# Attention's reads of PSUM traced with a raised priority

## The chip, the cores and the metric

The kernel runs on one core of one Trainium2 chip. The metric is the device time of one execution in microseconds (us); lower is better. Engines are named as the profile names them: PE (TensorE, matmuls), DVE (VectorE), ACT (ScalarE), POOL (GpSimd) and SP (SyncE, which here only issues DMAs). PSUM is the memory that matmuls write; it is split into banks of 512 float32 per partition.

## The reference

Two parts follow each other: causal attention with a bias, and a layer that mixes tokens by a Fourier transform and then applies an MLP. Cut to what matters:

```python
scores = q @ k^T / sqrt(D)                            # 8 batches, 8 heads, 576 tokens, D = 64
cum = cumsum(max(s, 0)); bias = -(cum[:, None] - cum[None, :])
scores = where(causal, -1e9, scores + min(bias, 0))
attn = exp(scores - max(scores)); attn /= sum(attn) + 1e-9
x = attn @ v                                          # heads side by side: (8, 576, 512)
u = x + real(fft(fft(x, axis=tokens), axis=features))
un = (u - mean(u)) / sqrt(var(u) + 1e-6)
out = u + relu(un @ w_ch1) @ w_ch2                    # 512 -> 2048 -> 512
```

The weights come in as float64 words, which the kernel turns into float32 and then into a high and a low part, so that three float32r matmuls give nearly float32 precision.

## The kernel before

Attention works on 32 pairs of heads (`i` = 0 to 31, four pairs to a batch). Each pair has generators: `high` and `low` split q and k into parts (L404, L420); `maxes` multiplies q by k in blocks of 128 queries and takes each row's maximum from PSUM with DVE (L456, read at L459 and L463), then transposes the maxima on PE (L468), copies them out with ACT (`mt`, L470) and sends them by DMA into a row of the next product; `scores` multiplies k by q with the bias and the maximum inside the product (L488, L489), and ACT takes the exponential out of PSUM into `P` (L492); `av` multiplies by V (L520), and ACT copies the product out (L523, L524, L526); `recip` inverts the row sums (L535, L536), sends them to DRAM (`rd`, L538) and reads them back spread over partitions (`rb`, L541); `finish` scales the product (`xa` or `xr`, L556) and moves part of it by DMA into `xs` (L558 to L560).

In the loop of L582 the generators of neighbouring pairs are woven: `scores(i)`, `av(i - 1)`, `maxes(i + 1)`, `high(i + 2)`, `recip(i - 2)` and `finish(i - 2)` run side by side. Every fourth pair a batch is complete, and `folds` forms sums and differences of it (`Aw`, `Bw`, `Df` on DVE and POOL; high and low parts `De`, `Do`, `eh` by a cast on ACT and a subtraction on DVE, through `split`, L67). `fourier` (L273) then runs its matmuls (pzs, pzc, pyc, pys) between those of attention, and adds the result into `xa` and `xs` on POOL (L321 to L324), from where DMAs write it to DRAM (L326 to L328).

The weights have 16 chunks. Six are converted to float32 during attention (`convert_w`, stored as `wD`); the other ten are converted in the first of nine MLP tiles, four quarters a chunk: L82, L84, L86 and L87 on DVE, L83 and L111 on ACT, L88 on POOL, and L113 half on DVE and half on POOL. An MLP tile is 16 steps of 24 matmuls (L182, and L195 to L197 one step later), with a relu on ACT (`zh`, L186) and its remainder on DVE (`zl`, L187) between. `ln_tile` prepares the tokens of a tile (L126 to L159); its last step on DVE is a reciprocal over 128x512 (L158).

What sets the order: each engine works through one queue in order. The order is made when the kernel is built. For PE it is the written order from L581 to L636 (`manual_schedule`), so through the whole attention loop. For DVE, ACT, POOL and SP a scheduler chooses among the instructions that it holds ready, by a priority that counts up as instructions are traced; the lower number goes first. The pools decide who waits: exponentials and Fourier products share three banks (`ps`), maxima and products with V five (`psm`).

Of the kernel before, what the change touches and what calls it, by code (L numbers as in the profile page):

```python
# [10 lines left out]
AF = mybir.ActivationFunctionType  # L11
ALU = mybir.AluOpType
# [3 lines left out]
AX = mybir.AxisListType  # L16
# [9 lines left out]
NEG = -1.0e30  # L26
# [3 lines left out]
N0 = 3  # L30
N1 = 8
WEXP = 0x38000000 + (20 << 20)

# key chunks: (keys, first query of the product, queries of the product, first query kept)
CH = [(128, 0, 576, 0), (128, 128, 448, 128), (128, 256, 320, 256), (128, 320, 256, 384), (64, 320, 256, 512)]
# [5 lines left out]
def fused_kernel(ctx, tc, qkT, vA, sP, wP, tabD, tabS, corr, out):  # L41
# [23 lines left out]

    # ---------------------------------------------------------------- MLP
    def split(dst_h, dst_l, src):  # L67
# [5 lines left out]
    def rounded(pool, f, x, bufs):  # L73
        """256 columns of chunk f of both weights, from the words of their float64, rounded to nearest: generates, returns the f32."""
        m = pool.tile([128, WC], I32, tag="wm", name="wm", bufs=bufs)
        raw = pool.tile([128, 2 * WC], I32, tag="raw", name="raw", bufs=bufs)
        nc.sync.dma_start(out=raw, in_=wP[f, :, WC * x:WC * x + WC].bitcast(I32))
        hi = raw.rearrange("p (n w) -> p n w", w=2)[:, :, 1]
        lo = raw.bitcast(U16).rearrange("p (n w) -> p n w", w=4)[:, :, 1]
        yield 0.0  # L80
        e = pool.tile([128, WC], I32, tag="we", name="we", bufs=bufs)
        nc.vector.tensor_scalar(e, hi, 0x7FF00000, None, op0=ALU.bitwise_and)  # L82
        nc.scalar.activation(e, e, AF.Relu, bias=wbias, scale=8.0)  # L83
        nc.vector.tensor_scalar(m, hi, 0xFFFFF, 0x100000, op0=ALU.bitwise_and, op1=ALU.bitwise_or)  # L84
        yield 0.4
        nc.vector.scalar_tensor_tensor(out=e, in0=hi, scalar=-0x80000000, in1=e, op0=ALU.bitwise_and, op1=ALU.bitwise_or)  # L86
        nc.vector.scalar_tensor_tensor(out=m.bitcast(F32), in0=lo, scalar=2.0 ** -16, in1=m, op0=ALU.mult, op1=ALU.add)  # L87
        nc.gpsimd.tensor_mul(e.bitcast(F32), m.bitcast(F32), e.bitcast(F32))  # L88
        yield 0.4
        return e.bitcast(F32)  # L90

    def convert_w(pool, lo, hi, bufs):
        """Chunks lo..hi-1 as f32, into wD."""
        for f in range(lo, hi):
            for x in range(1024 // WC):
                m = yield from rounded(pool, f, x, bufs)
                nc.sync.dma_start(out=wD[f, :, WC * x:WC * x + WC], in_=m)
                yield 0.2

    def load_w(pool, f):  # L100
        """Chunk f of both weights in high and low parts: into W."""
        wh = pool.tile([128, 1024], F32R, tag=f"wh{f}", name=f"wh{f}")
# [13 lines left out]
    def spread_sum(t, name, n):  # L116
        """1/512 of the sum of t over the partitions, on every partition (PSUM)."""
        th = lnp.tile([128, TOK], F32R, tag="th", name="th")
        tl = lnp.tile([128, TOK], F32R, tag="tl", name="tl")
        split(th[:, :n], tl[:, :n], t[:, :n])  # L120
        m = bank(name)
        nc.tensor.matmul(m[:, :n], ones, th[:, :n], start=True, stop=False)
        nc.tensor.matmul(m[:, :n], ones, tl[:, :n], start=False, stop=True)
        return m

    def ln_tile(t0, n, lag):  # L126
        """Centred tokens in high and low parts, their mean and 1 / deviation: generates into LN."""
        u = lnp.tile([128, 4, TOK], F32, tag="u", name="u")
# [84 lines left out]

    # ---------------------------------------------------------------- Fourier mixing
    fft_ctx = ExitStack()
# [27 lines left out]
    def folds(b, xa, xs):  # L243
        """The even and odd parts of one batch; xa: rows 0..255 of x^T, xs: rows 512-p and 384-p."""
        De = [fft.tile([128, 2, 289], F32R, tag=f"De{i}", name=f"De{i}") for i in range(2)]
# [27 lines left out]
    def fourier(b, xa, xs):  # L273
        """Fourier mixing of one batch in place."""
        De, Do = folded.pop(b)
# [66 lines left out]

    # ---------------------------------------------------------------- attention
    attb_ctx, att_ctx, atop_ctx = ExitStack(), ExitStack(), ExitStack()
# [4 lines left out]

    # Products of width 128: rows 0..2 carry the running sum (high, low) and the maximum,  # L350
    # rows 3..63 are zero, rows 64..127 carry the high parts of q and k.
    R = NB * NH
# [51 lines left out]
    def high(i):  # L404
        """The high parts of q and k, the running sums, and no maximum yet."""
        st = sts[i]
# [13 lines left out]
    def low(i):  # L420
        """The low parts of q and k, each beside the high part of the same."""
        st = sts[i]
# [20 lines left out]
    def maxes(i):  # L443
# [4 lines left out]
        for h in range(2):  # L448
            for c in range(5):
# [4 lines left out]
                for x, (k0, n) in enumerate(parts):  # L454
                    p = psm.tile([128, 512], F32, tag="m", name="pm", bufs=5)
                    nc.tensor.matmul(p[:nq, :n], qy[:, h, 128 * c:128 * c + nq], ky[:, h, k0:k0 + n], start=True, stop=True)  # L456
                    if len(parts) > 1 and not x:
                        first = M1[:nq, h:h + 1]
                        nc.vector.tensor_reduce(out=first, in_=p[:nq, :n], axis=AX.X, op=ALU.max)  # L459
                    else:  # L460
                        n = nk - k0
                        m0 = 512 - 128 * c + k0
                        nc.vector.tensor_tensor_reduce(out=trash[:nq, :n], in0=p[:nq, :n], in1=amask[:nq, m0:m0 + n], scale=1.0,  # L463
                                                       scalar=first if x else NEG, op0=ALU.add, op1=ALU.max, accum_out=col)
                    yield 1.0
# [10 lines left out]
    def scores(i):  # L476
# [3 lines left out]
        for h in range(2):  # L480
            P = attb.tile([128, PW], F32, tag="P", name="P", bufs=4)
            st["P"].append(P)
            for c, (nk, q0, nq, qk) in enumerate(CH):
                ksl = slice(128 * c, 128 * c + nk)
                parts = [(0, 256), (256, 320)] if c == 0 else [(q0, nq)]
                for a, n in parts:
# [4 lines left out]
                    o = POFF[c] + lo - qk  # L491
                    nc.scalar.activation(P[:nk, o:o + a + n - lo], p[:nk, lo - a:n], AF.Exp, scale=0.125)  # L492
                    if c == 3:
# [9 lines left out]
    def av(i):  # L503
# [5 lines left out]
        for h in range(2):  # L509
            P = st["P"][h]  # L510
            vs = slice(64 * h, 64 * h + 128)
            for lo, n, tg in ((0, 256, "A"), (256, 320, "B")):
                p = psm.tile([128, 512], F32, tag="m", name="pav" + tg, bufs=5)
                cs = [c for c in range(5) if CH[c][3] < lo + n]
                for c in cs:
# [5 lines left out]
                    if c == cs[-1]:  # L521
                        if h:
                            nc.scalar.copy(r1[:, lo:lo + n], p[0:1, :n])  # L523
                            nc.scalar.copy(x[64:128, lo:lo + n], p[64:128, :n])  # L524
                        else:
                            nc.scalar.copy(x[:, lo:lo + n], p[:, :n])  # L526
                    yield 4 * w / 2.4
            # the sums of P, the second head's beside a row of their own
            nc.sync.dma_start(out=sums[16 * h:16 * h + 16], in_=r1 if h else x[64:65])
# [90 lines left out]

    # ---------------------------------------------------------------- MLP over all tokens
    zp = ctx.enter_context(pool("zp"))
# [49 lines left out]
def take(gen, quota):  # L672
    """The part of a generator up to a cost."""
    done = 0.0
# [24 lines left out]
def weave(*streams):  # L699
    """Runs generators side by side, each at the pace of its total cost."""  # L700
    for _ in mixed(*streams):
        pass
# [105 lines left out]
```

## Time and profile before

| What | us |
|---|---|
| Median of three timed runs | 1434.8 |
| Lowest and highest of them | 1433.98 and 1438.31 |
| Profiled execution, its span (the page gives no other time for it) | 1440.3 |
| PE busy in it | 1336.1 |
| DVE busy | 749.1 |
| POOL busy | 555.6 |
| ACT busy | 539.6 |

The profiled execution is one more run; it lies 5.5 us above the median of the timed ones. Attention starts its first exponentials at 25 us and takes about 17 us a pair; the last pair starts at 544 us. From there to 720 us the end of attention, the last Fourier mixing and the conversion of ten weight chunks overlap with the first MLP tile. From 720 us on PE runs the remaining eight tiles with hardly a gap. A row of the timeline gives start, duration, engine, line, operation, output<-input, sizes, and in brackets the idle time ahead of it with who ended it. A row of the waits gives who waited for whom, the total, how often, and the longest.

### The profile page before, as it was taken

To read this page: it belongs to the slowest core of one execution; us is meant where nothing else is said; L and a number is where in the kernel's file an instruction comes from. 1 tells how busy PE (TensorE), PEld (TensorE's weight loads), DVE (VectorE), ACT (ScalarE), POOL (GpSimd) and SP (SyncE) were. 2 spreads that over 40 slices of the span, in tenths; PEclk is the share of its full clock that TensorE was granted. 3 is DMA by queue.
4 is the path that set the end of the run, shared out by engine and by line. 5 is a ranking of instruction groups with operands and counts; after the bars stand their busy time and mean duration, and the time that the engine had idled before them with its cause. 6 is when DMAs were issued, how large, how long until landed. Compare 5 with 4: busy or idle time off the path is not lost.

```text
span 1440.3 us, 17967 instructions
## 1 busy us (share of the span) xinstructions
PE 1336.1 (93%) x6190; PEld 1073.6 (75%) x6190; DVE 749.1 (52%) x1684; ACT 539.6 (37%) x1211; POOL 555.6 (39%) x540
## 2 busy tenths in 40 slices
PE   4987989897989897998799999999999999999998
PEld 2766767686867685786588888888888888888886
DVE  6667676867676778789833332133321323212212
ACT  4775656565656557344412121121211212112110
POOL 6454465655555566565641400314013140123300
PEclk9998989999989998899899999999999999999999
DMA  8655556565655545533200000000000000000000
GB/s 216 163 144 145 156 151 176 145 163 168 154 158 140 164 118 166 172 119 116 94 23 30 30 30 8 22 30 30 30 8 22 30 30 30 8 22 0 30 0 30
DMA packets 78166, 124.98 MB, mean 87 GB/s; under 512 B 11256, under 2 KB 36185, under 8 KB 78075
## 3 DMA queue, kind: packets, MB, share of 16 engines
q1 hardware_dynamic: 75627, 119.83, 28.8%
q0 software_dynamic: 1632, 2.43, 0.9%
q10 hardware_dynamic: 816, 1.57, 0.3%
q8 instruction: 49, 0.80, 0.2%
q14 instruction: 42, 0.34, 0.1%
HBM read 76.78 MB, written 23.07 MB: 69 GB/s over the span
## 4 chain that ended last, share of the span: by engine, by line
PE 50%; DVE 7%; POOL 2%; DMA 1%; issue 1%; ACT 1%; SPq 0%; DVEq 0%; POOLq 0%; ACTq 0%
PE h L182 25%; PE acc L197 8%; PE acc L195 8%; PE acc L196 8%; POOL we L88 1%; DVE wm L87 1%; DVE wm L84 1%; DVE we L82 1%; DVE wl L113 1%; DVE we L86 1%; DVE ucl L147 0%; DVE Df L259 0%; POOL wl L113 0%; DMA raw<-in_wP_dram 0%; ACT wh L111 0%
## 5 line engine op out<-in xcount | busy, mean ns | idle before, releaser
L187 DVE SCALAR_TENSOR_TENSOR zl<-h,zh 128x512 fp32r<-128x512 f32 x144 | 98.7, 686 | 405.6 <-ACT zh L186 405.6
L186 ACT ACTIVATE zh<-h 128x512 fp32r<-128x512 f32 x144 | 85.9, 596 | 531.7 <-PE h L182 531.7
L197 PE MATMUL acc<-zl,wh 128*128 128x512 f32 x576 | 227.5, 395 | 3.9 <-DVE zl L187 3.9
L195 PE MATMUL acc<-zh,wh 128*128 128x512 f32 x576 | 227.8, 396 | 1.2 <-ACT zh L186 1.2
L196 PE MATMUL acc<-zh,wl 128*128 128x512 f32 x576 | 226.9, 394 | 0.0
L520 PE MATMUL pavB<-P,va 128*128 128x320 f32 (+2 forms) x640 | 201.7, 404 | 7.8 <-ACT stage L524 7.1
L456 PE MATMUL pm<-KQ 128*128 128x256 f32 (+4 forms) x384 | 159.5, 434 | 38.5 <-DVE Mx L463 16.2
L492 ACT ACTIVATE P<-ps 128x320 f32<-128x320 f32 (+4 forms) x384 | 144.9, 390 | 116.7 <-PE ps L489 111.9
L488 PE MATMUL ps<-KQ 128*128 128x256 f32 (+3 forms) x384 | 153.0, 401 | 21.6 <-ACT P L492 12.8
L182 PE MATMUL h<-uch,wh 128*128 128x512 f32 x576 | 159.2, 397 | 8.3 <-ACT wh L111 8.3
L182 PE MATMUL h<-uch,wl 128*128 128x512 f32 x576 | 157.9, 396 | 0.8 <-DVE wl L113 0.8
L182 PE MATMUL h<-ucl,wh 128*128 128x512 f32 x576 | 157.2, 394 | 0.0
L463 DVE CUSTOM_DVE_ANT_0 trash<-pm,amask 128x128 bf16<-128x128 f32 (+3 forms) x256 | 123.8, 484 | 39.8 <-PE pm L456 23.3
L211 POOL TENSOR_TENSOR o<-o,w 128x512 f32<-128x512 f32 x32 | 41.6, 1301 | 251.6 <-issue 217.8
L182 PEld LDWEIGHTS h<-uch,wh 128*128 128x128 f32 x576 | 107.8, 189 | 35.8 <-ACT wh L111 11.9
L197 PEld LDWEIGHTS acc<-zl,wh 128*128 128x128 f32 x576 | 108.8, 189 | 30.9 <-DVE zl L187 5.8
L520 PEld LDWEIGHTS pavB<-P,va 128*128 128x128 f32 (+1 forms) x640 | 107.5, 198 | 32.4 <-issue 12.5
L182 PEld LDWEIGHTS h<-uch,wl 128*128 128x128 f32 x576 | 108.7, 189 | 26.6 <-DVE wl L113 1.5
L195 PEld LDWEIGHTS acc<-zh,wh 128*128 128x128 f32 x576 | 108.7, 189 | 26.4 <-ACT zh L186 2.1
L182 PEld LDWEIGHTS h<-ucl,wh 128*128 128x128 f32 x576 | 108.9, 189 | 24.7
L196 PEld LDWEIGHTS acc<-zh,wl 128*128 128x128 f32 x576 | 108.8, 189 | 24.8
L489 PE MATMUL ps<-q,k 128*128 128x256 f32 (+3 forms) x384 | 120.9, 317 | 1.4 <-POOL q L435 1.4
(139 smaller groups left out, 2035.1 us busy)
## 6 DMA issues: line engine op xcount, KB each, us to landing
qk<-in_qkT_dram SPq DMA_DIRECT2D x32, 576.0 KB
raw<-in_wP_dram SPq DMA_DIRECT2D x64, 256.0 KB
va<-in_vA_dram SPq DMA_DIRECT2D x32, 480.0 KB
q<-KQ SPq DMA_DIRECT2D x32, 288.0 KB
k<-KQ SPq DMA_DIRECT2D x32, 288.0 KB
rb<-rd SPq DMA_DIRECT2D x64, 144.0 KB
u<-uD SPq DMA_DIRECT2D x8, 1024.0 KB
out_dram<-o SPq DMA_DIRECT2D x32, 256.0 KB
```

Source lines behind the costliest of these rows:

```text
L182: nc.tensor.matmul(h[:, :n], a[:, j * 128:(j + 1) * 128], b[:, j, :n], start=i == 0, stop=i == 11)
L186: nc.scalar.activation(zh[:, :n], h[:, :n], AF.Relu)
L187: nc.vector.scalar_tensor_tensor(out=zl[:, :n], in0=h[:, :n], scalar=0.0, in1=zh[:, :n].bitcast(F32), op0=ALU.max, op1=ALU.subtract)
L195: nc.tensor.matmul(acc[j][:, :n], a[:, cs], y[:, :n], start=g == 0, stop=False)
L196: nc.tensor.matmul(acc[j][:, :n], b[:, cs], y[:, :n], start=False, stop=False)
L197: nc.tensor.matmul(acc[j][:, :n], a[:, cs], z[:, :n], start=False, stop=g == NF - 1)
L456: nc.tensor.matmul(p[:nq, :n], qy[:, h, 128 * c:128 * c + nq], ky[:, h, k0:k0 + n], start=True, stop=True)
L463: nc.vector.tensor_tensor_reduce(out=trash[:nq, :n], in0=p[:nq, :n], in1=amask[:nq, m0:m0 + n], scale=1.0, scalar=first if x else NEG, op0 ...
L488: nc.tensor.matmul(p[:nk, :n], ky[:, h, ksl], qy[:, h, a:a + n], start=True, stop=False)
L489: nc.tensor.matmul(p[:nk, :n], k1[:, h, ksl], q1[:, h, a:a + n], start=False, stop=True)
L492: nc.scalar.activation(P[:nk, o:o + a + n - lo], p[:nk, lo - a:n], AF.Exp, scale=0.125)
L520: nc.tensor.matmul(p[:, a - lo:n], va[:nk, c, vs], P[:nk, o:o + w], start=c == 0, stop=c == cs[-1])
```

## The change

The reads of PSUM in `maxes`, `scores` and `av` are traced inside `tc.high_priority(offset=AHEAD)`, which lowers their priority number by 400, as if they had been traced 400 instructions earlier. No instruction is added or taken away, and no size, buffer or wait in the code changes. Comments were taken out too.

```diff
+AHEAD = 400
...
                     if len(parts) > 1 and not x:
                         first = M1[:nq, h:h + 1]
-                        nc.vector.tensor_reduce(out=first, in_=p[:nq, :n], axis=AX.X, op=ALU.max)
+                        with tc.high_priority(offset=AHEAD):
+                            nc.vector.tensor_reduce(out=first, in_=p[:nq, :n], axis=AX.X, op=ALU.max)
                     else:
...
-                        nc.vector.tensor_tensor_reduce(out=trash[:nq, :n], in0=p[:nq, :n], in1=amask[:nq, m0:m0 + n], scale=1.0,
-                                                       scalar=first if x else NEG, op0=ALU.add, op1=ALU.max, accum_out=col)
+                        with tc.high_priority(offset=AHEAD):
+                            nc.vector.tensor_tensor_reduce(out=trash[:nq, :n], in0=p[:nq, :n], in1=amask[:nq, m0:m0 + n], scale=1.0,
+                                                           scalar=first if x else NEG, op0=ALU.add, op1=ALU.max, accum_out=col)
...
-                    nc.scalar.activation(P[:nk, o:o + a + n - lo], p[:nk, lo - a:n], AF.Exp, scale=0.125)
+                    with tc.high_priority(offset=AHEAD):
+                        nc.scalar.activation(P[:nk, o:o + a + n - lo], p[:nk, lo - a:n], AF.Exp, scale=0.125)
...
-                        if h:
-                            nc.scalar.copy(r1[:, lo:lo + n], p[0:1, :n])
-                            nc.scalar.copy(x[64:128, lo:lo + n], p[64:128, :n])
-                        else:
-                            nc.scalar.copy(x[:, lo:lo + n], p[:, :n])
+                        with tc.high_priority(offset=AHEAD):
+                            if h:
+                                nc.scalar.copy(r1[:, lo:lo + n], p[0:1, :n])
+                                nc.scalar.copy(x[64:128, lo:lo + n], p[64:128, :n])
+                            else:
+                                nc.scalar.copy(x[:, lo:lo + n], p[:, :n])
```

In the changed file the lines stand 2 to 6 lower (L259 is L261, L463 is L467, L541 is L547). The queues differ in few places: a swap or two in pairs 3, 4 and 6, some twenty rows on DVE and ACT around pairs 14 and 26 (the same rows in both), and from pair 30 on, where all engines but PE differ up to the end of the first MLP tile. PE's order is the same up to the MLP, where the pieces of the last Fourier mixing stand elsewhere between the same matmuls.

The first place is DVE's queue around pair 14, where the maxima of pair 15 meet the folds of a batch. Before:

```order
L463 ISA trash,Mx_126<-pm,amask 128x512
L463 ISA Mx_126 128x1
L255 TENSOR_TENSOR Df<-Aw 128x289
L459 TENSOR_REDUCE M_2690<-pm 64x1
L250 TENSOR_TENSOR Aw<-xa,xs 128x576
L69 TENSOR_TENSOR De_2740<-Df,De_2739 128x289
L463 ISA trash,Mx_126<-pm,amask,M_2690 64x320
L463 ISA Mx_126 64x1
L259 TENSOR_TENSOR Df<-Bw 128x288
L262 TENSOR_TENSOR e<-xs 1x288
L263 COPY e<-xs 1x1
L69 TENSOR_TENSOR Do_2742<-Df,Do_2741 128x288
```

and the same stretch of DVE's queue in the changed kernel:

```order
L467 ISA trash,Mx_126<-pm,amask 128x512
L467 ISA Mx_126 128x1
L462 TENSOR_REDUCE M_2690<-pm 64x1
L257 TENSOR_TENSOR Df<-Aw 128x289
L467 ISA trash,Mx_126<-pm,amask,M_2690 64x320
L467 ISA Mx_126 64x1
L252 TENSOR_TENSOR Aw<-xa,xs 128x576
L264 TENSOR_TENSOR e<-xs 1x288
L71 TENSOR_TENSOR De_2740<-Df,De_2739 128x289
L265 COPY e<-xs 1x1
L261 TENSOR_TENSOR Df<-Bw 128x288
L267 TENSOR_TENSOR eh<-e,eh 1x289
```

The last two reads of the maxima have moved ahead of Df, Aw and De, and the second Df (from `Bw`) now stands behind the slow row of one partition (e).

The second place is SP's queue at the end of attention, where the sums of the last pair go out (rd) and come back spread (rb). Before:

```order
L541 DMA rb<-rd 64x576 x2
L538 DMA rd<-sums 32x36
L97 DMA wD<-we 128x256
L541 DMA rb<-rd 64x576
L558 DMA xs<-xr 112x576
L559 DMA xs<-xr 15x576
L560 DMA xs<-xr 1x16x36
L327 DMA uD<-xs 128x576
L541 DMA rb<-rd 64x576
L326 DMA uD<-xa 128x2x576
L328 DMA uD<-xs 128x576
```

and the same stretch of SP's queue in the changed kernel:

```order
L547 DMA rb<-rd 64x576 x2
L99 DMA wD<-we 128x256
L564 DMA xs<-xr 112x576
L565 DMA xs<-xr 15x576
L566 DMA xs<-xr 1x16x36
L329 DMA uD<-xs 128x576
L544 DMA rd<-sums 32x36
L328 DMA uD<-xa 128x2x576
L330 DMA uD<-xs 128x576
L547 DMA rb<-rd 64x576 x2
```

The last pair's rd has moved behind the three DMAs of `xr` of the pair before and the first uD, and both of its rb behind all three uD.

The third place is DVE's queue over the same time, up to the scaling of the last pair (xr). Before:

```order
L298 CAST z_91<-zc_6291 96x1
L298 CAST z_92<-zc_6292 96x1
L535 TENSOR_SCALAR sums<-sums 32x36
L536 RECIPROCAL sums<-sums 32x36
L158 RECIPROCAL r<-r 128x512
L86 SCALAR_TENSOR_TENSOR we<-raw,we 128x256
```

and in the changed kernel, from the same casts on:

```order
L300 CAST z_91<-zc_6291 96x1
L300 CAST z_92<-zc_6292 96x1
L160 RECIPROCAL r<-r 128x512
L88 SCALAR_TENSOR_TENSOR we<-raw,we 128x256
L115 TENSOR_TENSOR wl_6327<-wl_6327,wh_6326 128x512
L71 TENSOR_TENSOR zs_6294<-pzs,zs_6293 96x256
L71 TENSOR_TENSOR zc_6292<-pzc,zc_6291 96x258
L300 CAST z_91<-zc_6291 96x1
L541 TENSOR_SCALAR sums<-sums 32x36
L300 CAST z_92<-zc_6292 96x1
L135 TENSOR_TENSOR t_7504<-u 128x512
L542 RECIPROCAL sums<-sums 32x36
```

The reciprocal of the last pair's sums has moved behind the long reciprocal of `ln_tile`. Further on, two zl (L187) have moved ahead of xr, and the third from inside the folds to the place between xr and the first Aw.

## The prediction

> **What bounds the kernel now.** I first cut the span into stretches of the windows view, each with busy time (and instructions) of PE, PEld, DVE, ACT and POOL, then the granted clock, the DMA share and GB/s. The two pairs in which the order differs within the attention loop come first, then the end of attention, then the MLP.
>
> ```profile
> 245.00:283.00 38.00, 30.05 (x163) 23.33 (x161) 30.09 (x77) 21.50 (x55) 23.77 (x25) 0.99 0.56 154
> 453.00:494.00 41.00, 33.06 (x167) 25.95 (x166) 31.05 (x78) 22.83 (x57) 24.93 (x26) 0.92 0.51 145
> 544.00:600.00 56.00, 49.66 (x216) 39.74 (x217) 43.01 (x73) 28.73 (x66) 33.11 (x32) 0.84 0.55 176
> 600.00:660.00 60.00, 55.71 (x259) 45.45 (x259) 54.12 (x123) 26.64 (x62) 34.71 (x40) 0.94 0.38 128
> 660.00:720.00 60.00, 46.58 (x163) 33.03 (x162) 55.95 (x113) 27.04 (x59) 37.37 (x39) 0.89 0.32 103
> 720.00:1440.00 720.00, 714.64 (x3098) 581.14 (x3096) 207.74 (x271) 125.66 (x213) 153.22 (x114) 1.00 0.06 22
> ```
>
> After 720 us PE is busy 714.64 of 720 us: half the span has no gap worth a search, and no read of attention in it. Whatever the change does, it does before 720, and it counts only if the moment moves at which PE's last stretch begins. That moment is set just before, in 660 to 720, where PE is busy 46.58 of 60 us and DVE 55.95. The waits of PE there say for whom:
>
> ```profile
> PE h L182 <- ACT wh L111: 8.3, 7, 2.3
> PE acc L197 <- DVE zl L187: 3.9, 3, 2.7
> ```
>
> PE waits 8.3 us in seven pieces for chunks of weights (ACT's cast is the last step of a conversion that is mostly DVE's work) and 3.9 us for remainders that stand in DVE's queue. So between 600 and 720 the end is set by DVE's queue: it holds the folds of the last batch, the remainders of its Fourier mixing and the conversions. DVE is idle in it for 60 - 54.12 + 60 - 55.95 = 9.9 us. What reaches DVE later at 590 us reaches 720 later, unless those 9.9 us take it up; what PE saves before 590 counts only through what it delivers to DVE and SP.
>
> In the loop of attention PE's order is written out and stays as it was. DVE is idle 7.9 of 38 us there, PE 7.95, so neither alone fills the time; they take turns.
>
> **The change part by part.** First, nothing is added or removed: every duration below stays, and only queue places change. Where the order of an engine is the same before and after (the pairs outside 14, 26 and the end, but for a few swaps of neighbours), I cost the change at 0. Bounds: a swap delays one of two instructions by the other, and such rows are 0.4 to 0.8 us (the casts and remainders below), on engines with 7 us of idle time a pair; I keep 0.5 us both ways for these swaps together.
>
> Second, pairs 14 and 26. PE's waits in the two stretches that end with a read that moved:
>
> ```profile
> PE pm L456 <- DVE Mx L463: 1.7, 2, 0.9
> ...
> PE ps L488 <- ACT P L492: 0.9, 1, 0.9
> PE pmt L468 <- DVE Mx L463: 0.7, 1, 0.7
> PE pm L456 <- ACT stage L524: 0.7, 1, 0.7
> ```
>
> and from the answer for 453 to 494:
>
> ```profile
> PE ps L488 <- ACT P L492: 0.9, 1, 0.9
> PE pm L456 <- ACT stage L524: 0.7, 1, 0.7
> ...
> PE pmt L468 <- DVE Mx L463: 0.4, 1, 0.4
> ```
>
> The most that can go is their sum, 1.7 + 0.9 + 0.7 + 0.7 = 4.0 us and 0.9 + 0.7 + 0.4 = 2.0 us. What the new order does with them I read from DVE's and ACT's timeline of pair 14:
>
> ```profile
> 254.78 1.07 DVE L255 TENSOR_TENSOR Df<-Aw 128x289 f32<-128x289 f32 x1
> 255.76 0.41 DVE L459 TENSOR_REDUCE M<-pm 64x1 f32<-64x256 f32 x1
> ...
> 257.13 0.53 DVE L463 CUSTOM_DVE_ANT_0 trash<-pm,amask,M 64x320 bf16<-64x320 f32 x1
> ...
> 257.61 1.20 DVE L259 TENSOR_TENSOR Df<-Bw 128x288 f32<-128x288 f32 x1
> 258.72 1.67 DVE L262 TENSOR_TENSOR e<-xs 1x288 f32<-1x288 f32 x1
> ```
>
> ```profile
> 260.49 0.43 ACT L264 CAST eh<-e 1x289 fp32r<-1x289 f32 x1 [1.06 <-DVE e L263]
> 260.82 0.42 ACT L492 ACTIVATE P<-ps 128x320 f32<-128x320 f32 x1
> 262.49 0.43 ACT L68 CAST De<-Df 128x289 fp32r<-128x289 f32 x1 [1.25 <-DVE Df L255]
> 262.83 0.33 ACT L492 ACTIVATE P<-ps 128x192 f32<-128x192 f32 x1
> ```
>
> The reduction over the last block changes places with Df, so it starts at 254.78 instead of 255.76 and the last maximum is out about 0.9 us sooner: the 0.7 us of the transposition (pmt) goes. DVE itself is almost without a gap here, so the same work ends at the same time, and the second Df comes behind e (1.67 us) instead of ahead of it. On ACT the cast of that Df therefore comes later, and the exponential over 320 stands behind the chain from e: at about 261.2 instead of 260.82 (an estimate: e's cast at 260.49 moves with e). The exponential over 192 no longer stands behind the cast of De that had waited 1.25 us. I take half of the 0.7 us as kept, since the next exponential is later by 0.4: -0.35 us a pair, **-0.7 us** for both. Bounds: +0.5 us each, when only the later exponential counts, and -4.0 and -2.0 us when all the waits go.
>
> Third, the end of attention. Four rows of 546 to 573 us show what the new order takes away:
>
> ```profile
> 546.14 4.56 DVE L259 TENSOR_TENSOR Df<-Bw 128x288 f32<-128x288 f32 x1
> ```
>
> ```profile
> 550.73 0.43 ACT L68 CAST Do<-Df 128x288 fp32r<-128x288 f32 x1 [4.11 <-DVE Df L259]
> ```
>
> ```profile
> 551.93 0.33 PE L488 MATMUL ps<-KQ 128*64 128x256 f32 x1 [1.50 <-ACT P L492]
> ...
> 572.17 0.50 PE L122 MATMUL var<-th,ones 128*128 128x512 f32 x1 [1.92 <-ACT th L68]
> ```
>
> A Df of 288 columns takes 4.56 us, where the same one of pair 14 above took 1.20 us; ACT holds its cast for 4.11 us, and the exponentials behind that cast come so late that PE stands for 1.50 us. In the new order the cast stands behind the exponentials and copies, so the 1.50 us goes. The 1.92 us ahead of the matmul of the variance is shortened at most; I take 0.7 of it. So PE, and POOL behind its Fourier results, run 2.2 us ahead by 580 us. Bounds: 0 (the stall falls on the next matmul) and 1.50 + 1.92 = 3.4 us.
>
> Against it stands SP's queue, whose instructions only issue, but in order:
>
> ```profile
> 574.29 1.14 SPq L541 DMA_DIRECT2D rb<-rd  x2
> 576.52 0.33 SPq L538 DMA_DIRECT2D rd<-sums  x1
> ...
> 587.67 0.33 SPq L327 DMA_DIRECT2D uD<-xs  x1
> 588.05 0.49 SPq L541 DMA_DIRECT2D rb<-rd  x1
> ```
>
> ```profile
> 576.52 3.50 DMA rd<-sums
> ...
> 588.05 3.32 DMA rb<-rd
> ```
>
> ```profile
> 591.49 0.76 DVE L556 TENSOR_TENSOR xr<-stage,rb 128x576 f32<-128x576 f32 x1 [3.35 <-DMA rb<-rd]
> ```
>
> Before, rd goes out at 576.52, and one rb behind L327 is what the last pair's xr waits for. Now rd stands behind L327 and both rb behind the last uD. L327 moves with the lead: 587.67 - 2.2 = 585.5; rd is issued 0.33 later at 585.8 and lands 3.50 later at 589.3; the first rb goes out then, the second 0.57 later (1.14 for two), and 3.32 later, at 593.2, xr may start: **+1.7 us** against 591.49. Bounds by the lead: with 3.4 us it is +0.5, with none +3.9.
>
> The last pair's reciprocal of sums moved behind a long one on DVE, and two zl and a third changed places with the folds:
>
> ```profile
> 576.42 3.28 DVE L158 RECIPROCAL r<-r 128x512 f32<-128x512 f32 x1
> ...
> 595.55 0.76 DVE L250 TENSOR_TENSOR Aw<-xa,xs 128x576 f32<-128x576 f32 x1 [1.55 <-DMA xs<-xr]
> ...
> 600.33 0.68 DVE L187 SCALAR_TENSOR_TENSOR zl<-h,zh 128x512 fp32r<-128x512 f32 x1
> ```
>
> The long reciprocal ends at 579.7, six us before rd is issued, so it hides the moved one completely; if L327 came out before 580 it would begin to decide. The third zl, 0.6 us net of overlap, now lies in the 1.55 us in which DVE waits for xs, so the queue behind the folds is shorter by 0.6. Net 1.7 - 0.6 = **+1.1 us** at the last conversion. Bounds: 0, if the 9.9 us of DVE's idle time take it up, and +3.9.
>
> Sum: -0.7 + 1.1 = +0.4 us, so 1440.3 becomes 1440.7 in the profiled execution. The median of the timed runs lies 5.5 us below this execution, so I put the 0.4 us on the median: 1434.8 + 0.4 = 1435.2 us.
>
> One rule bears on the stretch in which PE gets ahead:
>
> ```profile
> 572.50:586.20 13.70, 12.04 (x46) 10.52 (x46) 12.10 (x21) 6.14 (x13) 8.27 (x8) 0.50 0.45 140
> ```
>
> The granted clock there is 0.50 for 13.7 us although PE is busy 12.04 of them and the wait ahead of it was 1.92 us. The Trainium skill, "TensorE: Matmul & The Clock Gate", section "Part 1: The HAM clock gate (the "warmup" mystery)", says that the clock halves after at least one idle window of about 3.4 us; by that page no wait of 1.92 us matters to the clock and the sum stays. The trace does not agree: its half clock follows shorter waits than that.
>
> **The rivals.** *Nothing happens.* PE's order is the written one, and most pairs have the same rows on every engine; then the swaps and the lead are taken up by the idle 9.9 us of DVE, and the time is 1434.8. For it speaks that no single wait in pairs 14 and 26 exceeds 0.9 us; against it, that SP's rd moved by some 9 us.
>
> *Faster: all named waits of the two pairs go.* That is -4.0 - 2.0 = -6.0, and with +1.1 at the end 1434.8 - 4.9 = 1429.9 us. For it speaks that each of these rows names a read that now has priority; against it, that DVE has no gap around 255 to 263 us into which work could move, so that a wait removed comes back at the next exponential.
>
> *Faster: the clock.* If the lead of 2.2 us lets the half-clock stretch at 572 go, its 12.04 busy us become 6.0, the lead grows to 8.2, and L327 comes at 579.5. Then rd is issued at 579.8, lands at 583.3, the second rb is back at 587.2 and xr starts 4.3 us before its 591.49. With -0.6 and -0.7 that is -5.6, 1429.2 us. For it speaks that the half clock follows waits that shrink; against it, that the clock is below 1 in other stretches as well (0.92 from 453 to 494), so that a half-clock stretch may fall elsewhere as easily. The page named above would give it no chance, having no wait of 3.4 us to remove.
>
> *Slower: rd behind L327.* If PE's lead does not reach the Fourier results (POOL and DVE hold them up as before), L327 stays at 587.67, rd lands at 588.0 + 3.5 = 591.5 and xr starts at 595.4, +3.9. With the later exponentials, +0.5 in each of the two pairs, and the 0.5 of the swaps, the sum is +5.4, less 0.6 for the zl still +4.8: 1439.6 us. It decides where the lead is under about 0.5 us. For it speaks the row of L327, which waits for POOL, not PE; against it, the 1.50 us stall, which goes with certainty by the order.
>
> **How the numbers follow.** A measurement of this kernel can tell about 0.3%, 4.3 us, from no change: faster is under 1430.5, slower over 1439.1. The forecast (1435.2) gets 0.46 and "nothing" 0.16, both within 0.3%: 0.62. Faster: the two pairs 0.11 and the clock 0.07, together 0.18. Slower: rd behind L327 0.16, and 0.04 for a half-clock stretch more, which costs as much as one less gains (about +5.6, 1440.4): 0.20. The range reaches from the two faster cases to the slower ones, 1429.0 to 1440.5; what lies outside is a case with two of these at once.
>
> **What the profile of the changed kernel would show.** Right: 714 to 715 us of PE in the last 720; the pmt wait of pair 14 gone and the exponential over 320 later by 0.2 to 0.5 us; no Do cast with 4.11 us ahead of it near 550; PE two us ahead at 580; rd issued just after L327, at 585 to 586, and xr of the last pair at 592 to 594. Wrong: waits on exponentials gone in many pairs, which would mean that small swaps of neighbours decide; rd before 583 or after 587; another number of half-clock stretches; or a DVE queue that ends its last conversion more than 4 us off, with nothing of the above to show for it.

## The result and the profile after

The changed kernel takes 1445.93 us (median of 4 runs, 1442.44 to 1448.02) against 1435.84 us (median of 4, 1433.98 to 1438.31): ratio 1.0073, 95% interval 1.0054 to 1.0093. It is 10 us **slower**; the forecast was no change, 1435.2 us, and the time lies outside the range. The span of its profiled execution is 1446.3 us.

The windows view of the changed kernel, for the stretches that the prediction shows (busy time of PE, PEld, DVE, ACT, POOL with instructions, then granted clock, DMA share, GB/s):

```profile
245.00:283.00 38.00, 32.01 (x168) 25.66 (x167) 30.49 (x75) 21.48 (x56) 23.65 (x24) 0.96 0.56 157
453.00:494.00 41.00, 32.91 (x180) 26.38 (x179) 32.90 (x81) 24.41 (x61) 27.26 (x28) 0.98 0.53 147
544.00:600.00 56.00, 47.05 (x215) 37.88 (x214) 38.12 (x63) 26.31 (x58) 29.95 (x29) 0.88 0.47 151
600.00:660.00 60.00, 52.59 (x239) 42.10 (x237) 52.37 (x114) 24.57 (x57) 32.51 (x36) 0.91 0.38 126
660.00:720.00 60.00, 43.05 (x159) 29.43 (x158) 57.80 (x122) 29.12 (x64) 36.14 (x41) 0.95 0.29 96
720.00:1440.00 720.00, 719.78 (x3110) 585.31 (x3111) 212.08 (x272) 125.86 (x215) 155.21 (x117) 1.00 0.06 23
```

PE is as full behind 720 as before: it is busy 719.78 of 720 us here, and the 714.64 us of before are all of the time up to its last matmul, which ends at 1434.65. The loss lies in the three rows from 544 to 720: PE does 2.6, 3.1 and 3.5 us less in them. Windows of fixed times cannot say where it went, since the work slides through them. So I cut both profiles at events instead: the first score matmul of the last pair (544.4 and 542.1), the last `yp` of batch 6 on DVE (587.7 and 587.8), the first `Aw` of the last folds (595.5 and 599.5), the last `yp` of batch 7 (638.4 and 641.4), the end of the last cast `wh` of the weights on ACT (708.2 and 714.7). `yp` (L320) is DVE's last step on a batch's Fourier products, which POOL then adds into `xa` and `xs`. Before:

```profile
544.40:587.70 43.30, 36.95 (x162) 29.39 (x161) 35.74 (x61) 25.96 (x59) 27.98 (x27) 0.79 0.54 171
587.70:595.50 7.80, 7.80 (x35) 6.30 (x34) 2.48 (x5) 1.20 (x2) 3.08 (x4) 1.00 0.60 208
595.50:638.40 42.90, 38.61 (x185) 31.51 (x184) 39.00 (x87) 18.32 (x42) 22.87 (x24) 0.92 0.38 123
638.40:708.20 69.80, 59.86 (x235) 44.72 (x234) 65.34 (x147) 32.13 (x74) 41.74 (x49) 0.95 0.36 115
```

and in the changed kernel:

```profile
542.10:587.80 45.70, 36.74 (x170) 29.51 (x169) 35.31 (x61) 26.20 (x59) 28.50 (x28) 0.84 0.50 159
587.80:599.50 11.70, 11.70 (x54) 9.67 (x53) 3.25 (x5) 1.80 (x3) 2.99 (x4) 1.00 0.45 152
599.50:641.40 41.90, 35.26 (x166) 28.77 (x165) 37.43 (x80) 17.52 (x41) 20.97 (x23) 0.88 0.36 121
641.40:714.70 73.30, 60.03 (x232) 42.88 (x231) 68.41 (x153) 32.41 (x74) 42.92 (x50) 0.98 0.34 113
```

The differences are +2.4, +3.9, -1.0 and +3.5 us, in all +8.8; from the last cast to the end it is 0.5 less. The profile of before starts its last pair 2.3 us later, so the two spans differ by 6.0 only. From the last `yp` of batch 6 to the last cast DVE is busy 106.8 of 120.5 us before (2.48 + 39.00 + 65.34) and 109.1 of 126.9 after: 4.1 us more idle, and 2.3 us more of work in 238 instead of 239 instructions. Where the loop ends is no evidence between two single executions: the kernel with the early rd below, which keeps the loop's order of before, starts its last pair at 535.3 instead of 544.4.

The +3.9 has its cause in SP's queue. The timeline of SP in the changed kernel:

```profile
585.80 0.55 SPq L566 DMA_DIRECT2D xs<-xr  x1
587.76 0.33 SPq L329 DMA_DIRECT2D uD<-xs  x1
588.19 0.37 SPq L544 DMA_DIRECT2D rd<-sums  x1
590.04 0.38 SPq L328 DMA_DIRECT2D uD<-xa  x1
590.82 0.33 SPq L330 DMA_DIRECT2D uD<-xs  x1
591.24 1.49 SPq L547 DMA_DIRECT2D rb<-rd  x2
```

and what stands behind it on DVE:

```profile
595.45 0.76 DVE L562 TENSOR_TENSOR xr<-stage,rb 128x576 f32<-128x576 f32 x1 [3.07 <-DMA rb<-rd]
...
599.51 0.76 DVE L252 TENSOR_TENSOR Aw<-xa,xs 128x576 f32<-128x576 f32 x1 [1.70 <-DMA xs<-xr]
```

rd goes out 0.43 us after the first uD, at 588.19 instead of 576.52, both rb after the third uD, and xr starts 7.7 us after the last yp instead of 3.8.

The +2.4 is in the stretch where the prediction saw a stall go. Rows of the changed kernel, from the timelines of DVE, ACT and PE (`th` is the high part of `t`, and `mu` the product that gives the mean):

```profile
545.76 3.33 DVE L135 TENSOR_TENSOR t<-u 128x512 f32<-128x512 f32 x1 [2.73 <-DMA u<-uD]
549.18 1.86 DVE L136 TENSOR_TENSOR t<-t,t 128x512 f32<-128x512 f32 x1
```

```profile
551.08 0.62 ACT L70 CAST th<-t 128x512 fp32r<-128x512 f32 x1 [4.46 <-DVE t L136]
```

```profile
551.75 0.80 PE L124 MATMUL mu<-th,ones 128*128 128x512 f32 x1 [3.71 <-ACT th L70]
```

The long instruction on DVE is still there. Before, it was Df (4.56 us while POOL ran rows of its own); now `t` of `ln_tile` stands at that place, waits 2.73 us for a DMA and takes 3.33 us, and Df follows it with 0.46:

```profile
551.45 0.46 DVE L261 TENSOR_TENSOR Df<-Bw 128x288 f32<-128x288 f32 x1
```

ACT waits 4.46 us for `t` where it had waited 4.11 for Df, and PE 3.71 where it had waited 1.50. The two waits that the prediction named did shrink, from 1.50 us to none and from 1.92 to 0.5, but others came: all waits that the profile names for PE in this stretch sum to 9.0 us instead of 6.3.

### The profile page after: what moved, and what is told of

The parts are those of the page before. It is cut to its first block, busy times and chain, and to the rows that moved or that the text cites. A ratio compares the mean times of both kernels' runs of the same rounds, so it can differ in the third digit from the quotient of the medians.

```text
span 1446.3 us, 17964 instructions
## 1 busy us (share of the span) xinstructions
PE 1332.2 (92%) x6190; PEld 1070.1 (74%) x6190; DVE 752.6 (52%) x1684; ACT 539.5 (37%) x1211; POOL 555.9 (38%) x540
## 4 chain that ended last, share of the span: by engine, by line
PE 51%; DVE 8%; POOL 2%; DMA 1%; issue 1%; ACT 1%; SPq 0%; DVEq 0%; POOLq 0%
PE h L184 24%; PE acc L199 8%; PE acc L197 8%; PE acc L198 8%; DVE wm L86 1%; DVE wm L89 1%; DVE we L84 1%; DVE we L88 1%; POOL we L90 1%; DVE wl L115 1%; DMA raw<-in_wP_dram 0%; DVE ucl L149 0%; POOL wl L115 0%; PE pavB L525 0%; DMA u<-uD 0%
## 5 line engine op out<-in xcount | busy, mean ns | idle before, releaser
L467 DVE CUSTOM_DVE_ANT_0 trash<-pm,amask 128x128 bf16<-128x128 f32 (+3 forms) x256 | 123.5, 482 | 36.2 <-PE pm L458 19.0
L525 PEld LDWEIGHTS pavB<-P,va 128*128 128x128 f32 (+1 forms) x640 | 107.4, 198 | 30.5 <-issue 12.5
L184 PEld LDWEIGHTS h<-ucl,wh 128*128 128x128 f32 x576 | 109.1, 189 | 24.8
```

What stands on the lines that cost most here:

```text
L184: nc.tensor.matmul(h[:, :n], a[:, j * 128:(j + 1) * 128], b[:, j, :n], start=i == 0, stop=i == 11)
L525: nc.tensor.matmul(p[:, a - lo:n], va[:nk, c, vs], P[:nk, o:o + w], start=c == 0, stop=c == cs[-1])
```

## The experiments

Theory A: that the last pair's rd stands behind the first uD in SP's queue makes xr and the folds late, and DVE's full queue carries that to the end. Rival B: the moved reads of PSUM lose by themselves, in the loop. Rival C: DVE's idle time takes up a late xr. Ratios are to the kernel before on the same chip, with 95% intervals.

### The raised priority in part of the loop

```diff
+    def ahead(kind, i):
+        return tc.high_priority(offset=AHEAD) if i < 30 else nullcontext()
...
-                        with tc.high_priority(offset=AHEAD):
+                        with ahead("max", i):
```

> The raised priority only for pairs 0 to 29; the reads of pairs 30 and 31 keep their old priority, and SP's queue has the last rd ahead of the first uD of batch 6, as before the change. Theory A (the loss is made at the end of attention, by the last pair's rd behind that uD on SP; the loop itself gains a little): about 1433 to 1436 us, ratio 0.998 to 1.001 to before. Rival B (the moved maxima and exponentials of the loop's pairs lose the time): 1440 us or more, most of the change's +10. Also looked at: xr of the last pair at about 589 to 592 us in A.

1438.75 us, ratio 1.0018 (1.0000 to 1.0036). xr starts 3.5 us after the last yp. Most of the loss is gone, with 30 of 32 pairs still at raised priority; a small rest is at the edge of what the interval tells. The time lies between what A and B expected. With `i < 28`, where only DVE's and ACT's order differs from before:

> The raised priority only for pairs 0 to 27: the order differs from before on DVE and ACT alone (pairs 14 and 26 and a few swaps), SP, POOL and PE have the order of before. Theory A (the loop's part is small): 1434 to 1438 us, ratio 0.998 to 1.001; my prediction's -0.7 us lies in it. Rival B (the loop's moved reads cost a part of the loss, the +2.6 us that the run with pairs 0 to 29 left): 1438 to 1440, ratio 1.0015 to 1.003. Rival D (the reads gain what the waits name, 6 us): under 1431.

1435.91 us, ratio 0.9993 (0.9974 to 1.0011). B falls for the loop, and so does the hope of 6 us: the interval ends at 0.9974, a gain of 3.7 us. In the profile of the changed kernel (with all pairs) the waits of 245 to 290 us show why nothing is gained there:

```profile
PE pm L458 <- DVE Mx L467: 4.0, 3, 1.8
PE ps L492 <- ACT P L497: 1.8, 1, 1.8
```

The rows of pmt and stage (0.7 each) are gone, and those of the maxima and exponentials grew from 1.7 and 0.9 to 4.0 and 1.8 (to 2.0 and 1.8 in the profile with pairs 0 to 27).

### The late rd alone

The kernel before, without any raised priority, with one DMA put behind another:

```diff
-        nc.sync.dma_start(out=rd, in_=sums)
+        with tc.issue_after(last_ud[0].ins) if i == NP - 1 else ExitStack():
+            nc.sync.dma_start(out=rd, in_=sums)
...
-        nc.sync.dma_start(out=uD[2, :, ts], in_=xs[:, 0])
+        last_ud[0] = nc.sync.dma_start(out=uD[2, :, ts], in_=xs[:, 0])
```

> The kernel before, with the last pair's rd put behind the first uD (L327) in SP's queue and nothing else asked for; no read of PSUM has a raised priority. Theory A: this alone makes the loss, xr of the last pair at 595 to 596 us instead of 591.5 and the time up by 5 to 10 us, 1441 to 1446, ratio 1.0035 to 1.007. Rival B (the reads' priority itself) and rival C (DVE's idle time of 9.9 us between 600 and 720 takes the delay up): no change, 1434 to 1437.

1445.59 us, ratio 1.0052 (1.0031 to 1.0073). SP's timeline is that of the changed kernel, and xr starts 8.0 us after the last yp (592.64 and 584.66):

```profile
584.09 0.33 SPq L327 DMA_DIRECT2D uD<-xs  x1
584.52 0.37 SPq L540 DMA_DIRECT2D rd<-sums  x1
587.17 0.38 SPq L326 DMA_DIRECT2D uD<-xa  x1
587.94 0.33 SPq L328 DMA_DIRECT2D uD<-xs  x1
588.35 1.51 SPq L543 DMA_DIRECT2D rb<-rd  x2
```

So one DMA's place makes 4.5 to 10.5 us without any change to the reads; C falls. In this is what the scheduler made of the late rd: up to xr the other queues are those of before, but two zl now stand ahead of xr on DVE, and PE's order in the first MLP tile is that of the changed kernel. The start of xr in absolute time (592.6) missed the expected 595 to 596, since this execution was 3 us earlier at the last yp.

### The early rd

```diff
-    recip(NP - 1)
+    with tc.high_priority(offset=400):
+        recip(NP - 1)
```

On the changed kernel:

> The changed kernel, with the last pair's recip at raised priority too, so that its rd stands ahead of the uD again and both rb as well; all reads of PSUM keep the raised priority. Theory A: the loss goes, 1432 to 1437 us, ratio 0.997 to 1.001; xr at 588 to 591. Rival B: stays at 1443 to 1447, ratio 1.005 to 1.008.

1438.21 us, ratio 1.0014 (0.9995 to 1.0033): the larger part of the loss is gone though every read keeps its raised priority. It is 1 us more than A expected. On the kernel before:

> The kernel before, with the last pair's recip at raised priority: both rb now ahead of the first uD on SP, none behind it. Theory A in its plain form says that xr may come as soon as rb lands, 580 + 0.6 + 3.3 = 584 us, behind yp at 587.7 on DVE; but xr's own DMAs to xs still stand behind the last uD (590.96), so they are issued at 591.3 instead of 592.3: gain 1 us, 1433 to 1436, ratio 0.997 to 1.000. Rival (the stretch behind xr decides, whatever xr does): no change either way; a gain of over 4 us, below 1431.5, would say that xr decides and not its DMAs.

1436.43 us, ratio 0.9999 (0.9982 to 1.0016). xr starts 0.4 us after the last yp, but Aw no sooner than before (8.2 us after it): xr's DMAs still stand behind the last uD.

### uD from another queue

```diff
-        nc.sync.dma_start(out=uD[2, :, ts], in_=xs[:, 0])
+        dma = nc.gpsimd if b == NB - 2 else nc.sync
+        dma.dma_start(out=uD[2, :, ts], in_=xs[:, 0])
```

and the same for the other two writes.

> The changed kernel, with the three uD writes of batch 6 issued from POOL's queue instead of SP's, so that rd, rb and the DMAs of xr have nothing of the Fourier mixing ahead of them on SP. Theory A (SP's order makes the loss): back to 1431 to 1437 us, ratio 0.996 to 1.001; from the last yp of batch 6 to the end 849 to 852 us instead of 858.5. Rival B: stays at 1443 to 1447.

1446.24 us, ratio 1.0071 (1.0048 to 1.0094): a miss. With the uD gone, rd did not come early. SP's timeline of this kernel:

```profile
581.39 0.55 SPq L565 DMA_DIRECT2D xs<-xr  x1
...
582.92 0.55 SPq L567 DMA_DIRECT2D xs<-xr  x1
583.58 0.51 SPq L545 DMA_DIRECT2D rd<-sums  x1
585.13 1.13 SPq L548 DMA_DIRECT2D rb<-rd  x2
```

It now stands behind the DMAs of the pair before, which wait for POOL, and is late all the same: 1.3 us ahead of the last yp, where it had been 11.2 ahead. Aw comes 9.7 us after the last yp. But xr comes 4.4 us after it, only 0.6 later than before, so that a late xr does not by itself account for a loss as large as the change's; POOL also issues three DMAs of 0.58 to 0.77 us here. The uD was one way for rd to be late, not the only one. On the kernel before, with batches 6 and 7 on POOL:

> The kernel before, with the uD writes of batches 6 and 7 issued from POOL's queue: on SP nothing of the mixing stands ahead of rb, of xr's DMAs or of the raw loads. Theory A: xr's way is free, from the last yp of batch 6 to the end 846 to 850 us instead of 852.6, and the time 1430 to 1434, ratio 0.996 to 0.999. Rival (DVE's and POOL's own work decides behind xr, and POOL pays for issuing): 1435 to 1439.

1439.41 us, ratio 1.0027 (1.0001 to 1.0053): a miss too. xr starts early, but beside POOL's work and POOL's own issuing the row grows from 0.76 to 2.97 us, and Aw comes 9.3 us after the last yp:

```profile
579.86 2.97 DVE L557 TENSOR_TENSOR xr<-stage,rb 128x576 f32<-128x576 f32 x1 [0.52 <-DMA rb<-rd]
...
588.21 0.76 DVE L250 TENSOR_TENSOR Aw<-xa,xs 128x576 f32<-128x576 f32 x1 [3.00 <-DMA xs<-xr]
```

### What the late folds cost behind Aw

After the late rd the stretch behind Aw lost time too. One reason could be the raw loads, which stand behind batch 7's uD on SP; in this kernel (the late rd, and the uD of batch 7 from POOL) nothing holds them:

> The kernel before with the late rd, as in the run of the late rd alone, but the uD writes of batch 7 issued from POOL, so that the raw loads behind them do not wait. From xr to the end the late rd alone took 852.1 us, the kernel before 848.8. If the raw loads held behind that uD make these 3 us: 849 to 850 from xr to the end, and 1439 to 1443 us, ratio 1.002 to 1.005. If the changed order of PE and DVE in the first MLP tile makes them: 851.5 to 853, and 1442 to 1446.

1445.75 us, ratio 1.0066 (1.0044 to 1.0088). Freeing the raw loads brought nothing back. DVE's wait for them is 1.0 us here and was 2.4 with the late rd alone. What POOL's issues cost in this kernel is not known apart, so that a small share of the raw loads is not excluded. To see whether a delay as such is enough, POOL copies rb onto itself ahead of xr, twice and four times, with rd as early as before:

```diff
+        if i == NP - 1:
+            for _ in range(2):
+                nc.gpsimd.tensor_copy(rb, rb)
         (nc.vector if i == NP - 1 else nc.gpsimd).tensor_mul(dst, st["x"], rb)
```

> The kernel before, with two copies of rb onto itself on POOL (idle there) ahead of the last pair's xr, in all about 2.6 to 3.6 us; SP keeps the order of before up to the folds, with rd ahead of the uD. Theory A' (a late xr costs its delay one for one, wherever the delay comes from): 1439 to 1440.5 us, ratio 1.0015 to 1.003, and xr 2.6 to 3.6 us later after the last yp of batch 6 than before (3.8). Theory A'' (a late xr costs more than its delay, since the loss of the late rd was +8 us for 4.2 us at xr): 1442 to 1445, ratio 1.004 to 1.006. Rival C (DVE's idle time takes it up): 1435 to 1437.

1442.42 us, ratio 1.0039 (1.0023 to 1.0055). The copies took 1.39 us for both, not the 2.6 to 3.6 that were expected:

```profile
588.42 1.39 POOL L558 COPY rb<-rb 128x576 f32<-128x576 f32 x2 [0.42 <-DMA rb<-rd]
```

So xr came only 1.0 us later after the last yp (4.8 against 3.8), and Aw 8.9 after it instead of 7.9. The time rose by 6 us.

> The same with four copies, 5.2 to 7.2 us. A': 1441.5 to 1444, ratio 1.0035 to 1.005. A'': 1447 to 1451, ratio 1.0075 to 1.010. C: under 1438.

1444.97 us, ratio 1.0050 (1.0031 to 1.0068), with Aw 10.3 us after the last yp; the time lies between the two ranges expected. Every kernel with a late Aw lost more than its delay, and not in proportion to it: by the ratios +1.0 us goes with 5.6 us, +2.4 with 7.2, and +3.9 to +4.2 (the change, and the two kernels with the late rd) with 7.5 to 10.5. The two kernels with uD from POOL do not fit a single price either: +1.4 goes with 3.9 us (0.1 to 7.6), +1.8 with 10.2.

### xr first

```diff
-    recip(NP - 1)
-    finish(NP - 1)
+    with tc.high_priority(offset=400):
+        recip(NP - 1)
+    with tc.issue_after(finish(NP - 1).ins):
+        deferred.pop()()
```

`deferred` holds the three uD writes of batch 6, so that they stand behind xr's DMAs.

> The kernel before, with the last pair's recip at raised priority and the three uD writes of batch 6 queued behind the DMAs of the last xr on SP: neither rd, rb nor those DMAs stand behind the mixing. By theory A the folds' first Aw starts about 5 us after the last yp of batch 6 instead of 7.9, so the gain is about 2.9 us: 1432 to 1434.5, ratio 0.997 to 0.999. Rival (the stretch behind xr decides, as the run of the early rd alone gained nothing): 1435 to 1438.

1436.52 us, ratio 0.9996 (0.9978 to 1.0014). Aw comes 6.2 us after the last yp, 1.7 sooner than before, and nothing is gained. DVE's waits from the last yp on (583.9 to 630 us) say where it went. Before, the first of these two rows was 0.5 us in 588 to 642, the second 0.9:

```profile
DVE zl L187 <- ACT zh L186: 6.3, 4, 2.0
DVE ym L319 <- PE pys L314: 1.8, 1, 1.8
```

DVE waits for relus that PE's first MLP steps have not delivered yet. On the changed kernel:

> The same on the changed kernel. Theory A: the loss goes and the same 2.9 us may be gained: 1431 to 1437, ratio 0.996 to 1.001. Rival B (the moved reads of PSUM lose by themselves): 1439 or more.

1439.51 us, ratio 1.0016 (0.9999 to 1.0033): the loss is gone but for a rest that one interval does not tell from nothing. The time lies in what B expected (1439 or more), so a small loss by the moved reads themselves may remain at the end of attention. No version here is faster than the kernel before by more than its interval.

All kernels in one table: the ratio; the time from the last pair's first score matmul to the last yp of batch 6; from there to Aw; from the same yp to the last cast; and how long DVE is busy and idle in that last stretch (us, one profiled execution each).

| Kernel | ratio | pair 31 to yp | yp to Aw | yp to last cast | DVE busy | DVE idle |
|---|---|---|---|---|---|---|
| before | 1 | 43.3 | 7.9 | 120.5 | 106.8 | 13.7 |
| before, early rd | 0.9999 | 43.3 | 8.2 | 119.1 | 107.4 | 11.7 |
| raised for pairs to 27 | 0.9993 | 44.3 | 7.7 | 118.4 | 107.0 | 11.4 |
| before, xr first | 0.9996 | 44.6 | 6.2 | 121.5 | 106.0 | 15.5 |
| raised for pairs to 29 | 1.0018 | 45.7 | 7.6 | 122.0 | 106.9 | 15.1 |
| change, early rd | 1.0014 | 45.7 | 7.4 | 120.0 | 106.9 | 13.1 |
| change, xr first | 1.0016 | 45.7 | 6.1 | 123.0 | 108.0 | 15.0 |
| before, uD from POOL | 1.0027 | 44.6 | 9.3 | 122.5 | 109.1 | 13.4 |
| two copies of rb | 1.0039 | 44.0 | 8.9 | 125.4 | 108.2 | 17.2 |
| four copies of rb | 1.0050 | 44.7 | 10.3 | 125.5 | 106.6 | 18.9 |
| late rd alone | 1.0052 | 46.0 | 12.0 | 128.1 | 109.5 | 18.6 |
| late rd, uD 7 from POOL | 1.0066 | 44.0 | 11.8 | 127.5 | 107.4 | 20.1 |
| change, uD from POOL | 1.0071 | 46.6 | 9.7 | 128.0 | 106.6 | 21.4 |
| the change | 1.0073 | 45.7 | 11.7 | 126.9 | 109.1 | 17.8 |

The six kernels from two copies of rb downwards, all at 1.0039 or more, need 125 to 128 us for the stretch that takes the others 118 to 123, and DVE is idle 17 to 21 us in it instead of 11 to 15.5.

The first column of times shows how far single executions differ. Nine kernels have the order of before in that stretch, but for the two rows of the last sums in two of them, and take 43.3 to 46.0 us (mean 44.3). The change and the three kernels made from it with all reads raised take 45.7 to 46.6 (mean 45.9). So of the +2.4 us about 1.6 is the order's by the means, an estimate with much spread, and none of the four is ahead.

## Why the prediction was wrong

**What bounds the kernel** held. PE is full behind 720, and the end is set by DVE's queue from 590 to 710; the waits of PE in 660 to 720 name the same two sources in the changed kernel:

```profile
PE h L184 <- ACT wh L113: 7.5, 8, 1.7
PE acc L199 <- DVE zl L189: 3.9, 4, 1.6
```

**Nothing in the swaps and little in pairs 14 and 26** held: the kernel with pairs 0 to 27 is at 0.9993, and -0.7 us lies within its interval, as does 0. The single step was not right: the pmt wait went as said, but the waits for maxima and exponentials grew. The bound for pair 26 also left out a row of its view:

```profile
PE pm L456 <- DVE Mx L463: 2.3, 1, 2.3
```

With it 4.3 us instead of 2.0 could have gone there, and the rival with all waits gone would have stood at 1427.6. The forecast did not use it.

**"So PE, and POOL behind its Fourier results, run 2.2 us ahead by 580 us"** is the step that failed. It took the 1.50 us stall as gone because the cast behind the long Df had moved, and put nothing in its place. The length of that row did not belong to Df: it belonged to the place beside POOL. In all nine kernels with the order of before Df takes 4.54 to 4.56 us there; in the four with the changed order `t` takes 2.90 to 3.33 after waiting about 3 us for its DMA, and Df 0.46. In the kernel with pairs to 29, where yet another row stands there, that one got the length:

```profile
536.59 4.79 DVE L71 TENSOR_TENSOR De<-Df,De 128x289 fp32r<-128x289 f32 x1 [0.42 <-ACT De L70]
```

In the changed kernel the cast behind `t` is what PE's matmul of the mean waits for, 3.71 us. Of the 2.2 us lead nothing came: a lead would have shown as about 41 to 42 us to the last yp, and the changed order took 45.7 to 46.6. Whether this place also makes the rest of 0.14 to 0.18% that the repaired versions show is open. They all take 45.7 us, but through different waits: PE's wait for the mean is 4.4 us with the early rd and 1.5 with xr first, and with pairs to 29 PE waits 3.8 us for exponentials instead. The kernel with the late rd alone takes 46.0 with the order of before.

**"+1.7 us" at xr** was worked out right from the wrong lead. With no lead the prediction's own bound is +3.9, and +3.9 was measured (7.7 us from the last yp to xr against 3.8). This is the mechanism of the slower rival: rd behind the first uD, with no lead at the Fourier results. It had 0.16, and its row (L327 waits for POOL) was in the prediction. The lead that the forecast needed rested on one stall; that stall went, as it was called certain to, and other waits came in its place. Two of the signs that were named as wrong came too: rd after 587 (588.19), and a last conversion more than 4 us off (714.7 against 708.2).

**"Net at the last conversion"** had the direction right and the size wrong. The idle time of DVE did not take the delay up, and the price was not one for one either: 3.9 us at Aw became 6.4 us at the last cast (120.5 to 126.9), of which 4.1 are idle time of DVE and 2.3 longer rows. The rival's +4.8 us was too small for this, and the range ended at 1440.5, below the 1445.93. Why a late Aw costs more than its delay stays open in part. Freeing the raw loads did not bring it back. In the profile of the changed kernel the waits of DVE from 588 to 642 show zl for zh 3.7 us (0.5 before) and ym, the step ahead of yp, for pys 2.0 (0.9 before). The same two rows before, then the rows of the changed kernel:

```profile
DVE zl L187 <- ACT zh L186: 0.5, 1, 0.5
DVE ym L319 <- PE pys L314: 0.9, 1, 0.9
```

```profile
DVE zl L189 <- ACT zh L188: 3.7, 3, 2.0
DVE xr L562 <- DMA rb<-rd: 3.1, 1, 3.1
DVE ym L321 <- PE pys L316: 2.0, 1, 2.0
```

So DVE waits longer for PE's results, directly or through ACT, while the folds are late. This is not the whole price: in the two kernels with copies of rb the zl row is 0.3 us and missing, and the loss is there. The order behind Aw changes too when the scheduler expects late folds: PE then has 36 acc matmuls ahead of the first pzs of batch 7 instead of 24. That is not the reason by itself, since the kernel with two copies of rb keeps 24 there and loses all the same; but no run here holds the whole order and moves the delay alone.

**The clock** was not the cause: the granted clock from the last pair to the end differs in both directions between the stretches (0.79 to 0.84, then 0.92 to 0.88, then 0.95 to 0.98).

## What to carry to other kernels

A priority moves more than the instructions that carry it: here four reads of PSUM moved one small DMA by 11.7 us in a queue that another engine's results hold up, and undoing that, with the reads left as they were, took back most of the loss. Read the order of the DMA queues first, look in each queue for what stands ahead of a transfer on the critical chain, and ask what that one waits for. And when a long row goes from the trace's place, ask whether the length belongs to the instruction or to the place; if to the place, price the instruction that comes to stand there.

## What the runs showed of the hardware

The product xr on DVE, with two inputs in SBUF, took 0.76 us in the changed kernel and 2.97 us beside POOL's instructions in the one with uD from POOL, and the time shows as busy, not as waiting. The Trainium skill, "SBUF — State Buffer", section "Who interferes with whom", says that a DVE instruction with two inputs in SBUF contends with a GpSimd instruction that reads SBUF; the trace agrees with it (also the 4.56 us of Df and the 3.33 us of `t`). At one place beside POOL's rows the length stayed whatever DVE had there: 4.54 to 4.56 us for Df in nine executions, 4.79 for De in one, 2.90 to 3.33 for `t` in four, and 0.46 for Df where it came later. Two executions with the same order up to the last pair reached it at 544.4 and at 535.3 us, so that single profiles of this kernel may differ by 9 us before anything changed has run; a difference between two profiles is better read between events.
